# Decode operations in PSUM, the angle's scaling on ScalarE, and g in h's PSUM bank, in an attention and two-layer-block kernel

## Chip, cores and metric

The kernel runs on one core of one Trainium2 chip. The metric is the device time of one launch in microseconds (us). The engines are TensorE (PE; PEld is its weight load), VectorE (DVE), ScalarE (ACT) and GpSimd (POOL); SyncE's queue (SP) issues nearly all transfers.

## What is computed

Three parts follow one another over 4608 tokens (8 batches of 576 tokens, 8 heads of 64, so 512 columns):

```python
# attention; keys and values first averaged over pools of 8 tokens, so 72 keys per head
k_p = k.reshape(B, H, Sp, 8, D).mean(axis=3)
v_p = v.reshape(B, H, Sp, 8, D).mean(axis=3)
attn = softmax(matmul(q, k_p.T) / sqrt(D))
x = matmul(attn, v_p)                    # -> [4608, 512]
# first block: w_in [512, 2048], w_out [2048, 512]
h = x @ w_in
g = h * cos(h)
y = g @ w_out
# second block: w_in [512, 1024], w_out [1024, 512]
h2 = y @ w2_in
solu = h2 * softmax(h2)
out = layer_norm(solu) * g_ln @ w2_out
```

## The kernel before

**Tiling.** The tokens go in 9 blocks of 512 (`NB`, index `j`), the 2048 hidden columns of the first block in 16 chunks of 128 (`NF`, index `f`). A step `n` is one pair `(j, f)`. In a step PE does `h_mm` (12 matmuls into one PSUM bank of the pool `ps_h`, which has two) and `y_mm` of the step two before (12 matmuls into four banks of `ps_y`). Each product is three matmuls on pairs of float32r parts (a high part, and a low part that holds the rest), so every operand is split into two.

**The chain of a step.** From h to g the functions `chain_a`, `chain_b`, `chain_c` do: L527 (DVE) scales h by 1/2pi into an integer, L532 (DVE) takes the whole turns off, L536 (ACT) is the sine; L541 (DVE) multiplies by h, which is the last reader of h's bank; L543 (ACT) copies g's high part, L547 (DVE) subtracts it for the low part. `chain_a` runs in its own step, `chain_b` and `chain_c` of a step run in the next one.

**Decoding the weights.** The weights come as float64 bits. Class `Chunk` turns 128x512 of them into two float32r parts in three stages: `s1` (ACT L94, L95), `s2` (DVE L100, L105, L110, then POOL L113) and `s3` (ACT L122, POOL L125). Class `Pipe` runs the stages of neighbouring chunks one step apart; `parts()` is a generator that gives the DVE operations of `s2` out one at a time, so that `chain_a` can put its own between them. The 32 chunks of the first block's weights are decoded during the attention of block 0 and the steps of block 0, two pipe steps in a step `n`. The second block's weights are decoded in block 8 (`pipe2`). The scratch tiles of the decode lie in the SBUF pool `s2p` (four buffers).

**Attention.** Block 0's attention stands alone at the start, written out by hand; the attention of block `j+1` is laid into the steps of block `j` by `slots()`: `sl[2f]` early in a step, `sl[2f+1]` late. Its PSUM tiles (`sc`, `eTp`, `eLp`, `xo`) come from `ps_a`, which has two banks. In f 1, 2, 9 and 10 the early slot has scores, in f 2 and 10 the late slot has the exponentials, f 3 and 11 have the normalizations (`norm`: DVE L395, L397, L398, then POOL L401, L406), f 5 and 13 the transposes and, where a batch from the third on begins, `prep_v` (POOL L289, ACT L295, POOL L296, ACT L300, DVE L301 to L307), f 6 and 7 and 14 and 15 the product with v. Keys and values are pooled by `kv_jobs`: on POOL (L194, L214, L228), for batch 0's keys on DVE (L206 to L209).

**Order.** All is under a manual schedule: each engine takes its instructions in program order, and the order of the calls in the step loop is the order on every queue:

```python
h_mm(j, f)
chain_b(*steps[n - 1])
parts = pipe.parts(); next(parts, None)
chain_a(j, f, parts)          # then, in block 0, the second pipe step around chain_c
for fn in sl[2 * f]: fn()
chain_c(*steps[n - 1])        # j > 0
y_mm(*steps[n - SK])          # SK = 2
for fn in sl[2 * f + 1]: fn()
```

Of the kernel before, what the change touches and what calls it, by code (L numbers as in the profile page):

```python
# [28 lines left out]
# High words of the float64 range [2^-127, 2^128 - ulp], read as float32.  # L29
# [5 lines left out]
def fused_kernel(ctx, tc, qT_d, kT_d, vN_d, vM_d, vL_d, w_in, w_out, w2_in, w2_out, g_ln, out):  # L35
    """qT_d [pair, (head d), token]; kT_d [batch, pair, (head d), (r key)];
    vN_d [batch < 2, 128-token tile, token, (head d)];
    vM_d [batch >= 2, pair, (head key<64), (r d)]; vL_d [batch >= 2, half, (head rep key>=64), (r d)];
    weights [chunk, row, col] as bits of float64; g_ln [row, chunk]."""
# [43 lines left out]
    class Chunk:  # L83
# [13 lines left out]
        def s2(self):  # L97
            hi, lw = self.raw[:, :, 1], self.raw[:, :, 0]
            t = self.t
            nc.vector.tensor_scalar(  # L100
                out=t.bitcast(F32), in0=t.bitcast(F32), scalar1=WORD_MIN, scalar2=WORD_MAX,
                op0=ALU.max, op1=ALU.min,
            )
            yield
            nc.vector.tensor_scalar(  # L105
                out=t, in0=t, scalar1=0x07FFFFFF, scalar2=3,
                op0=ALU.bitwise_and, op1=ALU.logical_shift_left,
            )
            yield
            nc.vector.scalar_tensor_tensor(  # L110
                out=t, in0=hi, scalar=-0x40000000, in1=t, op0=ALU.bitwise_and, op1=ALU.bitwise_or)
# [3 lines left out]
        def s3(self):  # L115
# [5 lines left out]
            # The high part needs only the high word's bits; the low part takes all the rest.  # L121
# [6 lines left out]
    class Pipe:  # L128
        """Decodes chunks in order in three stages, one step apart, loads running ahead."""
# [17 lines left out]
        def step(self):  # L147
            for _ in self.parts():
                pass

        def parts(self):
            """One step, in three parts between which other work may go."""
            last = self.two.pop(0) if self.two else None
            if self.one:
                c = self.one.pop(0)
                yield from c.s2()
                self.two.append(c)
            if last:
                last.s3()
# [24 lines left out]
    def kv_jobs(b, hf):  # L184
        """Loads of half the heads of batch b; each gives the job that sums the pools."""
# [11 lines left out]
        def k_job(i):  # L197
# [5 lines left out]
            def add():  # L203
                if b == 0:
# [29 lines left out]
    # The first two batches' values, which are wanted early, are pooled on the tensor engine.  # L234
# [77 lines left out]
    class Attn:  # L312
        """Attention of one token block. The first one, which has the chip to itself, takes its
        buffers from the ring of the weights."""
# [141 lines left out]
        def slots(self):  # L456
# [12 lines left out]
            for hf in range(2):  # L469
# [23 lines left out]
                # Keys of the first half come a block ahead, the rest as they are wanted.  # L493
# [30 lines left out]
    def chain_a(j, f, between=iter(())):  # L524
        ps = h_ps[j, f]
        t = gp.tile([P, BLK], F32, tag="t", name="t")
        nc.vector.tensor_scalar(  # L527
            out=t.bitcast(I32), in0=ps, scalar1=1.0 / TWO_PI, scalar2=0.25,
            op0=ALU.mult, op1=ALU.add,
        )  # L530
        next(between, None)
        nc.vector.scalar_tensor_tensor(  # L532
            out=t, in0=t.bitcast(I32), scalar=-TWO_PI, in1=ps, op0=ALU.mult, op1=ALU.add)
        for _ in between:
            pass
        nc.scalar.activation(out=t, in_=t, func=AF.Sin, bias=halfpi)  # L536
        g_t[j, f] = [t, None]

    def chain_b(j, f):
        t = g_t[j, f][0]  # L540
        nc.vector.tensor_tensor(out=t, in0=t, in1=h_ps.pop((j, f)), op=ALU.mult)  # L541
        g = g_t[j, f][1] = gp.tile([P, 2, BLK], F32R, tag="g", name="g")
        nc.scalar.copy(out=g[:, 0], in_=t)  # L543

    def chain_c(j, f):
        t, g = g_t[j, f]
        nc.vector.tensor_tensor(out=g[:, 1], in0=t, in1=g[:, 0].bitcast(F32), op=ALU.subtract)  # L547
# [45 lines left out]
    def h2_mm(t):  # L593
# [3 lines left out]
        # The first two tiles run beside the last block's y.  # L597
# [14 lines left out]
    # u = h2 e^(h2 - max); solu = u / sum, whose layer norm goes by the moments of u.  # L612
# [90 lines left out]
    with tc.manual_schedule():  # L703
# [22 lines left out]
        # A raw buffer serves until the tile that takes over its slot: x or one of the last chunks.  # L726
# [90 lines left out]
        for n in range(len(steps) + SK):  # L817
            if n < len(steps):
# [12 lines left out]
                h_mm(j, f)  # L831
            if 0 < n <= len(steps):
# [3 lines left out]
            if n < len(steps):  # L836
                parts = pipe.parts()
                next(parts, None)
                chain_a(j, f, parts)
            parts = pipe.parts()  # L840
            if j == 0:
                next(parts, None)
                if n > 0:
                    chain_c(*steps[n - 1])
            if n < len(steps):
                if sl:
                    for fn in sl[2 * f]:
                        fn()
                if j == 0 and f in (4, 6):
                    kv_load(1, 1, KV[f // 2 - 2])  # L850
                if j == 0 and f in (5, 7):
                    add(1, 1, KV[f // 2 - 2])
            if j > 0 and n <= len(steps):
                chain_c(*steps[n - 1])
            if n < len(steps):
                for _ in parts:
# [96 lines left out]
```

## Time and profile before

| quantity | value |
|---|---|
| median of 3 runs | 1426.53 us (1426.36 to 1426.8) |
| span of the profiled execution, first to last instruction | 1422.4 us |
| mean granted TensorE clock | 0.982 |
| DVE busy | 981.3 us (69%) |
| ACT busy | 532.0 us (37%) |
| POOL busy | 403.4 us (28%) |

The profiled execution has no time of its own beside its span; 4.1 us of the median lie outside that span. Busy is time in which the engine had an instruction of the program in work; matmuls are pipelined and their ends are modelled, so a busy PE is not PE at its peak. A row that names a DVE operation by its line can be long because it computes or because it waits inside the engine.

### The profile page before, as it was taken

Reading aid. Unit: us, or ns where it says so; the run is one execution under the profiler, and the core shown is the slowest. Engines: PE = TensorE matmul, PEld = TensorE weight load, DVE = VectorE, ACT = ScalarE, POOL = GpSimd, SP = SyncE. Lnnn points to the kernel's source line nnn. Section 1 sums busy time; section 2 is a strip of 40 time slices with the busy share of each in tenths; the row PEclk is TensorE's granted clock in tenths of the full one; section 3 lists DMA queues with packets and bytes.
Section 4 is the critical chain, followed back from the end, with each engine's and each line's share of the span. In section 5 each row is a group of like instructions: output and inputs, shape, how many; then the busy total and the mean of one; then the engine's idle time right before and its main releaser. Section 6 shows DMA issues by size and latency. Waiting matters only on the chain.

```text
span 1422.4 us, 17189 instructions
## 1 busy us (share of the span) xinstructions
PE 1356.9 (95%) x6304; PEld 1117.5 (79%) x6304; DVE 981.3 (69%) x1690; ACT 532.0 (37%) x891; POOL 403.4 (28%) x517
## 2 busy tenths in 40 slices
PE   6778799999999999999999999799899999999998
PEld 4556588888888888888888888578788888888887
DVE  8999966666676666666656655697766666666664
ACT  5665533333343333333324333454222222222222
POOL 3787823231242142142231100353111111111110
PEclk9999999999999999999999999899999999999999
DMA  7433111111020120220110101340111111111100
GB/s 266 147 91 138 57 61 54 31 61 46 32 84 24 60 71 9 75 63 31 47 60 8 45 1 60 104 133 8 60 39 55 40 54 38 52 40 50 44 32 30
DMA packets 43236, 85.27 MB, mean 60 GB/s; under 512 B 4112, under 2 KB 13328, under 8 KB 43152
## 3 DMA queue, kind: packets, MB, share of 16 engines
q1 hardware_dynamic: 43008, 84.16, 18.0%
q8 instruction: 50, 0.82, 0.2%
q14 instruction: 34, 0.28, 0.1%
q10 hardware_dynamic: 144, 0.00, 0.0%
HBM read 65.28 MB, written 18.87 MB: 59 GB/s over the span
## 4 chain that ended last, share of the span: by engine, by line
PE 82%; DVE 12%; issue 2%; DMA 1%; ACT 1%; POOL 1%; SPq 0%; DVEq 0%; ACTq 0%; POOLq 0%
PE y L557 24%; PE h L519 23%; PE o L675 5%; PE o L677 5%; PE o L676 5%; PE h L608 4%; PE h L610 4%; PE h L609 4%; PE lT L661 2%; PE sc L351 2%; DVE dec L110 2%; DVE dec L105 2%; DVE dec L100 1%; DVE t L532 1%; PE eTp L431 1%
## 5 line engine op out<-in xcount | busy, mean ns | idle before, releaser
L519 PE MATMUL h<-x,wi 128*128 128x512 f32 x1728 | 427.5, 397 | 20.7 <-DVE t L541 20.7
L557 PE MATMUL y<-g,wo 128*128 128x512 f32 x1728 | 427.5, 396 | 14.6 <-DVE yo L568 9.6
L519 PEld LDWEIGHTS h<-x,wi 128*128 128x128 f32 x1728 | 328.1, 191 | 92.0 <-DVE t L541 24.3
L557 PEld LDWEIGHTS y<-g,wo 128*128 128x128 f32 x1728 | 323.2, 190 | 83.3 <-DVE yo L568 10.8
L527 DVE TENSOR_SCALAR t<-h 128x512 int32<-128x512 f32 x144 | 99.0, 688 | 157.3 <-PE h L519 157.2
L536 ACT ACTIVATE t<-t,cst 128x512 f32<-128x512 f32 x144 | 104.3, 724 | 230.5 <-DVE t L532 230.1
L543 ACT CAST g<-t 128x512 fp32r<-128x512 f32 x144 | 89.1, 618 | 188.8 <-DVE t L541 182.9
L194 POOL TENSOR_TENSOR kvraw<-kvraw 128x256 f32<-128x256 f32 (+3 forms) x128 | 86.9, 679 | 235.2 <-DMA kvraw<-in_vM 176.2
L648 POOL TENSOR_TENSOR sc<-sc,cst 128x1 f32<-128x1 f32 x36 | 19.8, 549 | 366.5 <-DVE sc L647 208.1
L675 PE MATMUL o<-wi,lh 128*128 128x512 f32 x288 | 116.0, 403 | 0.0
L676 PE MATMUL o<-wi,lh 128*128 128x512 f32 x288 | 112.9, 392 | 0.0
L677 PE MATMUL o<-wi,ll 128*128 128x512 f32 x288 | 112.9, 392 | 0.0
L547 DVE TENSOR_TENSOR g<-t,g 128x512 fp32r<-128x512 f32 x144 | 109.4, 760 | 1.8 <-ACT g L543 1.8
L663 ACT CAST lh<-lT 128x512 fp32r<-128x512 f32 x72 | 38.8, 589 | 184.6 <-PE lT L661 184.6
L401 POOL TENSOR_TENSOR em<-e,sm 128x512 f32<-128x512 f32 x34 | 39.6, 1165 | 229.3 <-PE y L557 220.1
L617 DVE TENSOR_REDUCE sc<-h 128x1 f32<-128x1024 f32 x34 | 41.6, 1224 | 90.8 <-PE h L610 90.8
L113 POOL TENSOR_TENSOR dec<-dec,raw 128x512 int32<-128x512 int32 x48 | 69.0, 1438 | 118.2 <-DVE dec L110 52.2
L532 DVE SCALAR_TENSOR_TENSOR t<-t,h 128x512 f32<-128x512 int32 x144 | 98.7, 686 | 4.4
L541 DVE TENSOR_TENSOR t<-t,h 128x512 f32<-128x512 f32 x144 | 97.1, 675 | 5.6 <-ACT t L536 5.2
L610 PE MATMUL h<-wi,yl 128*128 128x512 f32 x216 | 84.2, 390 | 0.0
L608 PE MATMUL h<-wi,yh 128*128 128x512 f32 x216 | 84.1, 389 | 0.0
L609 PE MATMUL h<-wi,yh 128*128 128x512 f32 x216 | 84.1, 389 | 0.0
(139 smaller groups left out, 1904.2 us busy)
## 6 DMA issues: line engine op xcount, KB each, us to landing
raw<-in_w_in SPq DMA_DIRECT2D x24, 512.0 KB, 3.6
raw<-in_w_out SPq DMA_DIRECT2D x24, 512.0 KB, 3.5
kvraw<-in_kT SPq DMA_DIRECT2D x32, 288.0 KB, 2.8
qT<-in_qT SPq DMA_DIRECT2D x36, 256.0 KB, 3.3
yd<-yo SPq DMA_DIRECT2D x36, 256.0 KB, 2.8
yr<-yd SPq DMA_DIRECT2D x18, 512.0 KB, 3.7
out<-o SPq DMA_DIRECT2D x36, 256.0 KB, 2.0
kvraw<-in_vM SPq DMA_DIRECT2D x24, 256.0 KB, 2.6
```

Source lines behind the costliest of these rows:

```text
L519: nc.tensor.matmul(ps, lhsT=w[:, a, kk, :], rhs=x[kk][:, b], start=(kk == 0 and i == 0), stop=(kk == KD - 1 and i == 2),)
L527: nc.vector.tensor_scalar(out=t.bitcast(I32), in0=ps, scalar1=1.0 / TWO_PI, scalar2=0.25, op0=ALU.mult, op1=ALU.add,)
L532: nc.vector.scalar_tensor_tensor(out=t, in0=t.bitcast(I32), scalar=-TWO_PI, in1=ps, op0=ALU.mult, op1=ALU.add)
L536: nc.scalar.activation(out=t, in_=t, func=AF.Sin, bias=halfpi)
L547: nc.vector.tensor_tensor(out=g[:, 1], in0=t, in1=g[:, 0].bitcast(F32), op=ALU.subtract)
L557: nc.tensor.matmul(o, lhsT=w[:, a, P * e:P * (e + 1)], rhs=g[:, b], start=(f == 0 and i == 0), stop=(f == NF - 1 and i == 2),)
L608: nc.tensor.matmul(ps[hh], lhsT=hi[:, kk, c], rhs=w[:, 0], start=first, stop=False)
L609: nc.tensor.matmul(ps[hh], lhsT=hi[:, kk, c], rhs=w[:, 1], start=False, stop=False)
L610: nc.tensor.matmul(ps[hh], lhsT=lo[:, kk, c], rhs=w[:, 0], start=False, stop=last)
L675: nc.tensor.matmul(ps, lhsT=hi[:, c], rhs=w[:, 0], start=(c == 0), stop=False)
L676: nc.tensor.matmul(ps, lhsT=hi[:, c], rhs=w[:, 1], start=False, stop=False)
L677: nc.tensor.matmul(ps, lhsT=lo[:, c], rhs=w[:, 0], start=False, stop=(c == NF2 - 1))
```

## The change

- The first two DVE operations of `s2` write a PSUM tile `bits` from `ps_a` instead of the SBUF scratch tile; the third reads it and writes SBUF.
- A pipe step is issued whole, with `s3` of the older chunk ahead of `s2`; `parts()` is gone.
- L527 leaves DVE: a new `chain_k` scales h by an activation on ACT.
- `chain_b` writes the product back into h's PSUM bank; the copy of the high part reads it there, and `chain_c` subtracts from it there, so that `chain_c` is now the last reader of h's bank.
- In block 0 a step's order is `chain_b`, a pipe step, `chain_c`, `chain_k`, early attention, a pipe step, `chain_a`. In the other blocks it is `chain_b`, early attention, `chain_c`, `chain_k`, `chain_a`.
- For batch 0 only one of two keys' tiles of a half is pooled on DVE; the other goes to POOL (`add` in `k_job`).

```diff
         def s2(self):
...
+            b = ps_a.tile([P, BLK], I32, tag="a", name="bits")
             nc.vector.tensor_scalar(
-                out=t.bitcast(F32), in0=t.bitcast(F32), scalar1=WORD_MIN, scalar2=WORD_MAX,
+                out=b.bitcast(F32), in0=t.bitcast(F32), scalar1=WORD_MIN, scalar2=WORD_MAX,
                 op0=ALU.max, op1=ALU.min,
             )
-            yield
             nc.vector.tensor_scalar(
-                out=t, in0=t, scalar1=0x07FFFFFF, scalar2=3,
+                out=b, in0=b, scalar1=0x07FFFFFF, scalar2=3,
                 op0=ALU.bitwise_and, op1=ALU.logical_shift_left,
             )
-            yield
             nc.vector.scalar_tensor_tensor(
-                out=t, in0=hi, scalar=-0x40000000, in1=t, op0=ALU.bitwise_and, op1=ALU.bitwise_or)
+                out=t, in0=hi, scalar=-0x40000000, in1=b, op0=ALU.bitwise_and, op1=ALU.bitwise_or)
...
         def step(self):
-            for _ in self.parts():
-                pass
-
-        def parts(self):
-            """One step, in three parts between which other work may go."""
             last = self.two.pop(0) if self.two else None
+            if last:
+                last.s3()
             if self.one:
                 c = self.one.pop(0)
-                yield from c.s2()
+                c.s2()
                 self.two.append(c)
-            if last:
-                last.s3()
             self.fill()
...
             def add():
-                if b == 0:
+                if b == 0 and i == 0:
...
-    def chain_a(j, f, between=iter(())):
+    def chain_k(j, f):
         ps = h_ps[j, f]
         t = gp.tile([P, BLK], F32, tag="t", name="t")
-        nc.vector.tensor_scalar(
-            out=t.bitcast(I32), in0=ps, scalar1=1.0 / TWO_PI, scalar2=0.25,
-            op0=ALU.mult, op1=ALU.add,
-        )
-        next(between, None)
+        nc.scalar.activation(
+            out=t.bitcast(I32), in_=ps, func=AF.Copy, scale=1.0 / TWO_PI, bias=0.25)
+        g_t[j, f] = [t, None]
+
+    def chain_a(j, f):
+        t, ps = g_t[j, f][0], h_ps[j, f]
         nc.vector.scalar_tensor_tensor(
             out=t, in0=t.bitcast(I32), scalar=-TWO_PI, in1=ps, op0=ALU.mult, op1=ALU.add)
...
     def chain_b(j, f):
-        t = g_t[j, f][0]
-        nc.vector.tensor_tensor(out=t, in0=t, in1=h_ps.pop((j, f)), op=ALU.mult)
+        t, ps = g_t[j, f][0], h_ps[j, f]
+        nc.vector.tensor_tensor(out=ps, in0=t, in1=ps, op=ALU.mult)
         g = g_t[j, f][1] = gp.tile([P, 2, BLK], F32R, tag="g", name="g")
-        nc.scalar.copy(out=g[:, 0], in_=t)
+        nc.scalar.copy(out=g[:, 0], in_=ps)
 
     def chain_c(j, f):
-        t, g = g_t[j, f]
-        nc.vector.tensor_tensor(out=g[:, 1], in0=t, in1=g[:, 0].bitcast(F32), op=ALU.subtract)
+        g = g_t[j, f][1]
+        nc.vector.tensor_tensor(
+            out=g[:, 1], in0=h_ps.pop((j, f)), in1=g[:, 0].bitcast(F32), op=ALU.subtract)
...
+            early = sl[2 * f] if n < len(steps) and sl else []
+            late = sl[2 * f + 1] if n < len(steps) and sl else []
...
+            if n < len(steps) and j == 0:
+                pipe.step()
                 if n > 0:
                     chain_c(*steps[n - 1])
...
+                chain_k(j, f)
+                for fn in early:
+                    fn()
...
+                pipe.step()
+                chain_a(j, f)
+            else:
+                for fn in early:
+                    fn()
+                if n <= len(steps):
+                    chain_c(*steps[n - 1])
+                if n < len(steps):
+                    chain_k(j, f)
+                    chain_a(j, f)
```

## Rows read from the trace of the kernel before

**Rows 1.** Busy time by stretch: us, busy of each engine, granted clock, DMA share, GB/s

```profile
44.76:161.88 117.12, 89.81 (x368) 68.31 (x367) 115.89 (x163) 73.83 (x117) 89.86 (x72) 0.90 0.33 107
175.00:880.00 705.00, 704.25 (x3353) 584.88 (x3353) 450.08 (x784) 255.80 (x392) 178.41 (x310) 1.00 0.15 47
```

**Rows 2.** Groups of DVE, 44.76 to 161.88 us: count, busy us, mean ns

```profile
L105 DVE TENSOR_SCALAR dec<-dec 128x512 int32<-128x512 int32 x26 | 28.2, 1086 | 0.0
L110 DVE SCALAR_TENSOR_TENSOR dec<-raw,dec 128x512 int32<-128x512 int32 x27 | 25.8, 956 | 0.5
L100 DVE TENSOR_SCALAR dec<-dec 128x512 f32<-128x512 f32 x26 | 18.9, 728 | 0.2 <-ACT dec L94 0.2
L527 DVE TENSOR_SCALAR t<-h 128x512 int32<-128x512 f32 x13 | 8.8, 678 | 0.0
L371 DVE TENSOR_REDUCE mx<-sc 128x4 f32<-128x288 f32 x8 | 3.5, 444 | 0.0
```

**Rows 3.** Timeline: start us, us taken, engine, line

```profile
131.46 1.28 POOL L125 TENSOR_TENSOR wo<-dec,wo 128x512 fp32r<-128x512 f32 x1
131.99 1.03 DVE L105 TENSOR_SCALAR dec<-dec 128x512 int32<-128x512 int32 x1
...
906.42 0.43 DVE L105 TENSOR_SCALAR dec<-dec 128x512 int32<-128x512 int32 x1
```

**Rows 4.** Groups of ACT, 44.76 to 161.88 us

```profile
L536 ACT ACTIVATE t<-t,cst 128x512 f32<-128x512 f32 x13 | 9.4, 723 | 3.9 <-DVE t L532 3.9
```

**Rows 5.** Groups of POOL, 44.76 to 161.88 us

```profile
L113 POOL TENSOR_TENSOR dec<-dec,raw 128x512 int32<-128x512 int32 x26 | 39.6, 1522 | 27.3 <-DVE dec L110 12.8 <-ACT t L536 8.5 <-DMA raw<-in_w_out 3.4
```

**Rows 6.** Timeline of DVE: where steps 1 and 13 of block 0 begin

```profile
51.73 0.68 DVE L541 TENSOR_TENSOR t<-t,h 128x512 f32<-128x512 f32 x1
52.33 1.29 DVE L100 TENSOR_SCALAR dec<-dec 128x512 f32<-128x512 f32 x1
...
161.88 0.67 DVE L541 TENSOR_TENSOR t<-t,h 128x512 f32<-128x512 f32 x1
```

**Rows 7.** Timeline of block 4, steps f 3 to 6

```profile
504.71 1.29 POOL L401 TENSOR_TENSOR em<-e,sm 128x512 f32<-128x512 f32 x1 [3.58 <-PE y L557]
...
515.65 0.61 POOL L289 TENSOR_TENSOR vw<-v,cst 128x256 f32<-128x256 f32 x1
...
516.31 2.88 PE L519 MATMUL h<-x,wi 128*128 128x512 f32 x12
...
519.72 0.68 DVE L547 TENSOR_TENSOR g<-t,g 128x512 fp32r<-128x512 f32 x1
...
520.68 2.94 PE L557 MATMUL y<-g,wo 128*128 128x512 f32 x12
```

**Rows 8.** The line of `prep_v`'s first operation, all its instructions

```profile
L289 POOL TENSOR_TENSOR vw<-v,cst x12: 610/612/615, 216.1 to 758.6; 128x256 f32<-128x256 f32 x12
```

**Rows 9.** Timeline of block 4, step f 13 and after

```profile
566.65 2.88 PE L519 MATMUL h<-x,wi 128*128 128x512 f32 x12
...
...
570.76 2.95 PE L557 MATMUL y<-g,wo 128*128 128x512 f32 x12
```

**Rows 10.** Waits of PE, 840 to 1020 us: us in total, times, longest

```profile
PE h L519 <- DVE t L541: 3.4, 2, 2.6
```

**Rows 11.** A pause of PE, and stretches behind two pauses; columns as in group 1

```profile
1017.70:1021.70 4.00, 0.00 (x0) 0.03 (x1) 3.24 (x3) 0.00 (x0) 2.85 (x2) 1.00 0.00 0
1022.70:1025.50 2.80, 2.80 (x9) 2.22 (x8) 2.10 (x3) 1.95 (x4) 0.00 (x0) 0.50 0.00 0
928.50:931.50 3.00, 2.99 (x13) 2.46 (x14) 2.96 (x4) 2.23 (x4) 2.15 (x2) 1.00 0.43 139
```

**Rows 12.** Timeline of block 0's attention

```profile
13.44 0.76 POOL L406 TENSOR_TENSOR el<-e,sm 128x128 f32<-128x128 f32 x2
...
15.07 0.45 DVE L362 TENSOR_REDUCE mx<-sc 128x4 f32<-128x288 f32 x1
...
28.69 1.55 POOL L194 TENSOR_TENSOR kvraw<-kvraw 128x288 f32<-128x288 f32 x2
```

More of the change, by code (lines that the diff above doesn't have):

```diff
@@ L522, in h_mm @@
                 )
-    def chain_a(j, f, between=iter(())):
+    def chain_k(j, f):
         ps = h_ps[j, f]
         t = gp.tile([P, BLK], F32, tag="t", name="t")
-        nc.vector.tensor_scalar(
-            out=t.bitcast(I32), in0=ps, scalar1=1.0 / TWO_PI, scalar2=0.25,
-            op0=ALU.mult, op1=ALU.add,
-        )
-        next(between, None)
+        nc.scalar.activation(
[3 more added lines that the diff above has]
+        t, ps = g_t[j, f][0], h_ps[j, f]
         nc.vector.scalar_tensor_tensor(
             out=t, in0=t.bitcast(I32), scalar=-TWO_PI, in1=ps, op0=ALU.mult, op1=ALU.add)
-        for _ in between:
-            pass
         nc.scalar.activation(out=t, in_=t, func=AF.Sin, bias=halfpi)
-        g_t[j, f] = [t, None]
     def chain_b(j, f):
-        t = g_t[j, f][0]
-        nc.vector.tensor_tensor(out=t, in0=t, in1=h_ps.pop((j, f)), op=ALU.mult)
+        t, ps = g_t[j, f][0], h_ps[j, f]
+        nc.vector.tensor_tensor(out=ps, in0=t, in1=ps, op=ALU.mult)
         g = g_t[j, f][1] = gp.tile([P, 2, BLK], F32R, tag="g", name="g")
-        nc.scalar.copy(out=g[:, 0], in_=t)
+        nc.scalar.copy(out=g[:, 0], in_=ps)
     def chain_c(j, f):
-        t, g = g_t[j, f]
-        nc.vector.tensor_tensor(out=g[:, 1], in0=t, in1=g[:, 0].bitcast(F32), op=ALU.subtract)
+        g = g_t[j, f][1]
+        nc.vector.tensor_tensor(
+            out=g[:, 1], in0=h_ps.pop((j, f)), in1=g[:, 0].bitcast(F32), op=ALU.subtract)
     def y_mm(j, f):
@@ L835, in fused_kernel @@
                 y_out(*steps[n - SK - 1])
[L836 to L842, printed above, removed]
+            if n < len(steps) and j == 0:
+                pipe.step()
                 if n > 0:
                     chain_c(*steps[n - 1])
[L845 to L849, printed above, removed]
+                chain_k(j, f)
+                for fn in early:
+                    fn()
+                if f in (4, 6):
                     kv_load(1, 1, KV[f // 2 - 2])
-                if j == 0 and f in (5, 7):
+                if f in (5, 7):
                     add(1, 1, KV[f // 2 - 2])
[L853 to L856, printed above, removed]
-                    pass
+                pipe.step()
[8 more added lines that the diff above has]
+                    chain_a(j, f)
             if n >= SK:
@@ L860, in fused_kernel @@
             if n < len(steps):
-                if sl:
-                    for fn in sl[2 * f + 1]:
-                        fn()
+                for fn in late:
+                    fn()
                 if pipe2 and f > 0:
```

## The prediction

> **What bounds the kernel now.** I read the busy times by stretch first. From 175 to 880 us, which is blocks 1 to 7, PE is busy for 704.25 of 705.00 us at a granted clock of 1.00 [rows 1]: there every microsecond in which PE waits is added to the time, and work taken off DVE is worth nothing. From 44.76 to 161.88 us, block 0's steps beside the decode, DVE is busy for 115.89 of 117.12 us and PE for 89.81 [rows 1]: there DVE sets the pace. The groups of DVE in that stretch say what fills it: L105 takes 1.086 us in the mean, L110 0.956, L100 0.728, while L527, of the same size with its source in PSUM, takes 0.678 [rows 2]. The timeline shows why. With nothing on POOL beside it L105 takes 0.43 us; with L125 on POOL from 131.46 to 132.74 it takes 1.03 and ends at 133.02, 0.28 behind POOL's end [rows 3]. So much of DVE's busy time is waiting for POOL's instruction to be over.
>
> **The change, part by part.** The sum is made against the profiled span of 1422.4 us; 4.1 us of the median of 1426.5 lie outside it and are left alone.
>
> *Block 0's steps.* Step 1 begins with L541 at 51.73 and step 13 at 161.88 [rows 6], so twelve steps took 110.15 us. After the change no operation of the decode on DVE has two operands in SBUF, and neither has the chain of g. I take 0.68 us for each (L527's price, the nearest row with PSUM in it [rows 2]); the next operation starts 0.60 later (51.73 to 52.33 [rows 6]), or at the end plus 0.05 where it needs the result. A step without attention is then, in DVE's order: L541 0.60, a decode 2.06 (0.73, 0.73, 0.60), L547 0.60, a decode 2.06, L532 0.68; then the sine, 0.72 [rows 4] and 0.12 for two handings, because L541 of the next step now stands right behind. That is 6.85 us, in which DVE waits 0.8. ACT's nine operations of about 0.6 (the scaling of h among them) fit in, and POOL's four too, at the 1.3 us that L125 needs [rows 3] rather than the 1.52 of L113 [rows 5].
> Attention was hidden in the waits for POOL and now adds to DVE. Scores add four operations of 0.44 [rows 2]: 8.6 us for f 1, 2, 9, 10. In f 3 and 11 ACT has two exponentials and two table loads more, and L397 can still wait for POOL: 9.95. In f 4 and 12 POOL is behind with the normalizations and L94 waits for L113: 7.75. Copies on ACT that DVE waits for make 9.0 of f 5, 9.55 of f 6 and 7.9 of f 7; f 8 is 6.9. The sum is 103.15, so 7.0 us are gained, and 1.2 at the same rate in the last two steps with decode: **-8.2**. Lower bound: if the waits among ACT, POOL and DVE are hidden, -16. Upper bound: seven operations a step now write or read PSUM in a way for which there is no row; 0.1 us more for each takes it all, so 0. I take the value between because L527's row is of the same size and differs only in where it writes.
> Here the Trainium skill speaks against the change ("VectorE: DVE Perf Modes", section "Why PSUM operands drop a tier"): an operation with an operand in PSUM can't use both SBUF read ports for one tensor, so an fp32 scale runs at one element a cycle instead of two. The rows show the price, 0.43 for L105 in SBUF against 0.678 for L527. By that rule alone a decode would get 0.5 us longer; the means of 1.086 and 0.728 say that the fast form is rarely had here. It is rival 4 below.
>
> *The wait for h's bank.* `chain_c` now reads h's bank, so `h_mm` two steps on waits for L547, where before it waited for L541. L547 stands behind the early attention on DVE. In most steps it is there in time: the early work needs PE's short matmuls, and 2.72 us of y follow them. The exception is f 5 in the blocks where `prep_v` runs, which are six (L289 ran twelve times, twice a block [rows 8]). In block 4 h of f 6 started at 516.31, and L547 ran from 519.72 to 520.40 [rows 7]: at its old place it would hold h up for 4 us. It comes earlier, though. What L547 waits for begins with the normalization on POOL at 504.71 [rows 7], which waited behind L527 and L532; these now come after it, and before it stands the later exponential (the sine of f 2 now follows the scores). Together POOL starts 1.45 us earlier, and so does L289 behind its transfer: 514.2. From L289's start to L547's end were 4.75 us (515.65 to 520.40), and a handing to PE of 0.2 makes 519.15, 2.8 us after h could start. Before, y behind the attention's product started 0.74 late in that step (516.31 + 2.72 + 0.91 for the eight short matmuls is 519.94; it started at 520.68 [rows 7]). So the loss is 2.0 us in each of six blocks: **+12**. Bounds: +6 if L289 comes another microsecond earlier; +21 if the clock falls too (rival 3). Queued behind the waiting matmul is the attention's product, and behind that y, whose operands are all there.
>
> *f 13.* There L289 doesn't wait for a transfer, and ACT comes to `prep_v` before the scaling and the sine of its own step, so the product's operands are 3 us earlier. L547 ends about when h may start. What is gained is the late start of y: 570.76 against 566.65 + 2.72 + 0.91 = 570.28 [rows 9], 0.5 us in six blocks: **-3**. Bounds -4 and +3, the latter if L547 comes half a microsecond after h could start.
>
> *Block 8.* PE waited 3.4 us for L541, in two waits [rows 10], in the steps with two decodes each. With 2.06 us a decode, three operations of the chain and the wait for g's copy such a step takes DVE 6.8 us, against 5.44 of PE, so most but not all of the waiting goes: **-2.5**, bounds -3.4 and 0.
>
> *Block 0's attention.* The fourth tile of keys is now pooled on POOL, behind a normalization that ends there at 14.20 [rows 12]. Its two halvings (1.55 [rows 12]) and two small sums (0.75, an estimate by size) end at 16.5, the first scores at 17.3, where DVE's maximum stood at 15.07 [rows 12]: 2.2 late. The reduction that DVE saves falls into that wait, and the decode behind it is 0.5 longer. This stretch is bound by DVE, so I take **+2.5**; bounds 0, if later waits absorb it, and +5, if the three other decodes there add their 0.5 and PE resumes at the lower clock.
>
> Everything else is at nothing: in the blocks 1 to 7 the scaling on ACT and the shorter L547 are hidden behind PE, as ACT is busy for 255.80 of 705 us [rows 1]. If that cover went, the scaling's 0.7 us would stand between h and L532 in all 144 steps.
>
> The sum is -8.2 + 12 - 3 - 2.5 + 2.5 = +0.8: a span of 1423.2 and a time of **1427.3 us**, no change that shows (0.2% is 2.9 us, about what a measurement of this kernel can tell).
>
> **Rivals.**
> 1. *The wait for h's bank doesn't bite.* If the chain of normalization, transfer and `prep_v` ends 2.8 us earlier than I think, the +12 goes: 1415 to 1416. For it: half of that chain is waiting, for a transfer and for DVE's order. Against it: L547 was 4 us too late before, and two thirds of that must vanish.
> 2. *Block 0 gets much shorter.* DVE's waits for the sine and for ACT's copies overlap: -16 instead of -8.2, so 1419.5. For it: PE would allow it, with 89.81 us of work in 117.12. Against it: ACT and POOL come to 6 us and more in each step.
> 3. *The clock falls* (slower). After a pause of PE of 4.0 us the granted clock was 0.50, the lower level of 1.2 GHz, for 2.80 us; behind a wait of 2.6 us it stayed at 1.00 [rows 10, 11]. My pauses at f 5 are 2.8 us. If they make it fall, each costs 1.4 us more: 6 x 1.4 is 8.4, so 1435.7. It decides from a pause somewhere between those two.
> 4. *The fast form's loss is all that remains* (slower). If DVE's waits for POOL come back as waits for POOL's results (POOL was busy for 89.86 of 117.12 us [rows 1]), or an operation from PSUM to PSUM takes 0.1 us longer than L527, block 0 gains nothing: 1435.5. This is what the rule named above would give.
>
> **How the numbers follow.** My forecast has a chance of 0.40, with its own range of 1421 to 1433; of it 0.09 lies on the faster side of 0.2%, 0.22 within, 0.09 on the slower side. Rival 1 has 0.20, rival 2 0.12 (both faster), rival 3 0.14 and rival 4 0.14 (both slower). That makes 0.41 faster, 0.22 no change, 0.37 slower. The range goes to the middle of the rivals on each side, 1415 to 1437, and leaves out some 2 in 10.
>
> **What would show it.** Right: L100, L105 and L110 near 0.7 us each in block 0, however POOL is busy; twelve steps near 103 us; PE waiting for L547 (its line after the change) some 2.8 us, six times, ahead of h at f 6, and hardly at f 14; the first waits in block 8 gone; the maximum of the fourth scores near 17.3 us. Wrong: operations on PSUM that are longer than 0.75; `prep_v`'s L289 more than 2 us earlier against h; a granted clock below 1.00 in blocks 1 to 6; a loop over the sine longer than 7 us, or waits for the two banks of `ps_a`, which the decode now shares with the attention.

## The result and the profile after

The changed kernel took 1440.74 us (median of 4 runs, 1436.27 to 1441.45) against 1426.44 us of the kernel before beside it: a ratio of 1.0096, 95% interval 1.0079 to 1.0114. It is 1% slower. The profiled span grew from 1422.4 to 1439.6 us, by 17.2; the medians differ by 14.3. The two traces lie further apart because launches of one kernel differ: the spans of the kernel before, over all its launches, run from 1420.6 to 1427.2 us, so its trace is one of the short ones, and those of the changed kernel from 1434.5 to 1439.6, of which its trace is the longest. What is read from one trace against another is uncertain by a part of that. Of the 4.1 us put outside the span of before some 1.8 lie outside it (the changed kernel's traced launch took 1441.39 us with a span of 1439.6); the rest is that its trace is a short one.

Where the time went can be read from one instruction that stands once in every step in both kernels, the multiplication of the sine by h (L541 before, L536 after). This is its start after minus its start before, at the ends of the stages:

| at the multiplication of | step 1 | step 13 | block 1 begins | block 7 begins | block 8 begins | block 8 ends |
|---|---|---|---|---|---|---|
| start after minus start before, us | +3.88 | -4.53 | -3.90 | +19.41 | +19.44 | +17.12 |

Block 0's attention costs 3.9 us, the twelve steps behind it give back 8.4, the last steps of block 0 cost 0.6, blocks 1 to 6 cost 23.3, block 7 nothing, and block 8 gives back 2.3.

**Block 0.** The first view is the busy time by stretch, with columns as in [rows 1]: the twelve steps of block 0, and blocks 1 to 7.

```profile
55.61:157.35 101.74, 79.66 (x335) 62.38 (x336) 86.25 (x142) 73.71 (x121) 71.93 (x68) 0.92 0.36 113
175.00:880.00 705.00, 688.57 (x3244) 572.94 (x3243) 365.91 (x653) 307.49 (x489) 163.29 (x304) 0.98 0.14 43
```

DVE, busy for nearly all of its stretch before [rows 1], is busy for 86.25 of 101.74 us. In the second row PE has lost 16 us of its 705, and the granted clock is 0.98 where it was 1.00. The groups of DVE and POOL in the twelve steps answer to [rows 2, 5]:

```profile
L107 DVE TENSOR_SCALAR bits<-bits 128x512 int32<-128x512 int32 x24 | 16.8, 699 | 0.8
L111 DVE SCALAR_TENSOR_TENSOR dec<-raw,bits 128x512 int32<-128x512 int32 x24 | 16.5, 689 | 2.2
L103 DVE TENSOR_SCALAR bits<-dec 128x512 f32<-128x512 f32 x24 | 16.4, 685 | 0.0
...
L542 DVE TENSOR_TENSOR g<-h,g 128x512 fp32r<-128x512 f32 x12 | 8.2, 685 | 0.5 <-ACT g L538 0.5
...
L114 POOL TENSOR_TENSOR dec<-dec,raw 128x512 int32<-128x512 int32 x24 | 31.4, 1306 | 6.5 <-DVE dec L111 6.5
```

Each operation of a decode takes 0.69 to 0.70 us whatever POOL does, and POOL's addition takes 1.31 us instead of 1.52. The shortest, the median and the longest (ns) of the second operation in the twelve steps say it best, first before, then after:

```profile
L105 DVE TENSOR_SCALAR dec<-dec x24: 411/978/1520, 54.1 to 158.7; 128x512 int32<-128x512 int32 x24
L107 DVE TENSOR_SCALAR bits<-bits x24: 698/699/700, 56.9 to 154.5; 128x512 int32<-128x512 int32 x24
```

One of the prediction's signs of being wrong did show: the scores on PE (L347) wait 9.3 us in these steps for L111, that is for a bank of `ps_a` that the decode holds. The maxima L367 on DVE, which need the scores, stand 0.0 us, so no price of it shows. The timelines of DVE and POOL show the step starts, which answer to [rows 6], and the wait for the fourth tile of keys, which answers to [rows 12]:

```profile
55.61 0.70 DVE L536 TENSOR_TENSOR h<-t,h 128x512 f32<-128x512 f32 x1 [2.40 <-ACT t L531]
...
157.35 0.69 DVE L536 TENSOR_TENSOR h<-t,h 128x512 f32<-128x512 f32 x1 [0.79 <-ACT t L531]
...
17.61 0.46 DVE L358 TENSOR_REDUCE mx<-sc 128x4 f32<-128x288 f32 x1 [3.50 <-PE sc L347]
...
14.04 1.36 POOL L190 TENSOR_TENSOR kvraw<-kvraw 128x288 f32<-128x288 f32 x2
```

**Blocks 1 to 6.** PE's waits from 182 to 882 us hold one entry (total us, times, longest):

```profile
PE h L515 <- DVE g L542: 16.4, 6, 3.5
```

Block 4's timeline shows one of the six; it answers to [rows 7].

```profile
515.08 1.05 POOL L397 TENSOR_TENSOR em<-e,sm 128x512 f32<-128x512 f32 x1 [0.47 <-ACT t L531]
...
523.76 0.61 POOL L285 TENSOR_TENSOR vw<-v,cst 128x256 f32<-128x256 f32 x1
...
524.73 0.25 ACT L296 ACTIVATE vlh<-v 128x64 fp32r<-128x64 f32 x1
...
525.08 0.64 DVE L297 TENSOR_TENSOR vll<-v,vlh 128x64 fp32r<-128x64 f32 x1 [4.87 <-ACT vlh L296]
...
527.83 0.68 DVE L542 TENSOR_TENSOR g<-h,g 128x512 fp32r<-128x512 f32 x1
...
528.57 4.36 PE L515 MATMUL h<-x,wi 128*128 128x512 f32 x12 [2.21 <-DVE g L542]
```

Two things are to be seen. `prep_v` begins at 523.76 on POOL. DVE stands for 4.87 us before L297, with the subtraction L542 behind it, and h's matmuls wait 2.21 us for L542. And those twelve matmuls then take 4.36 us, where they took 2.88 before [rows 7]. The stretches behind the six pauses, columns as above, say why:

```profile
215.90:222.60 6.70, 5.92 (x16) 4.76 (x16) 2.02 (x4) 1.31 (x2) 2.37 (x6) 0.50 0.45 122
321.60:324.90 3.30, 3.30 (x9) 2.58 (x9) 1.05 (x2) 1.31 (x2) 0.00 (x0) 0.52 0.63 173
424.90:430.90 6.00, 6.00 (x16) 4.84 (x17) 1.18 (x2) 1.31 (x2) 1.55 (x4) 0.50 0.47 145
529.90:533.20 3.30, 3.30 (x10) 2.61 (x9) 0.69 (x1) 0.59 (x1) 1.44 (x3) 0.51 0.64 228
632.40:635.70 3.30, 3.21 (x8) 2.54 (x9) 1.32 (x3) 1.31 (x2) 0.38 (x2) 0.50 0.57 175
735.60:742.00 6.40, 6.40 (x30) 5.43 (x31) 2.79 (x5) 2.40 (x4) 1.71 (x4) 1.00 0.41 125
```

In five of six blocks PE worked at 0.50, the lower level of 1.2 GHz: 5.92 + 3.30 + 6.00 + 3.30 + 3.21 = 21.7 us of work, half of which, 10.9 us, would not have been needed at 1.00 if everything in it went at half the pace (an estimate, and an upper one: see e8). Block 6, with the shortest pause (2.10 us), kept 1.00. It is the natural control: from f 5 to f 9 it lost 2.0 us against before, the others 3.5 to 6.1.

**Block 8.** Of the two waits of [rows 10], 3.4 us, one is left:

```profile
PE h L515 <- DVE g L542: 1.3, 1, 1.3
```

### The profile page after: what moved, and what is told of

It reads as the page before. It is cut to its first block, busy times and chain, and to the rows that moved or that the text cites. A ratio compares the mean times of both kernels' runs of the same rounds, so it can differ in the third digit from the quotient of the medians.

```text
span 1439.6 us, 17090 instructions
## 1 busy us (share of the span) xinstructions
PE 1361.7 (95%) x6304; PEld 1124.8 (78%) x6304; DVE 867.7 (60%) x1540; ACT 608.2 (42%) x1035; POOL 381.4 (26%) x525
## 5 line engine op out<-in xcount | busy, mean ns | idle before, releaser
L515 PE MATMUL h<-x,wi 128*128 128x512 f32 x1728 | 434.5, 402 | 28.0 <-DVE g L542 28.0
L515 PEld LDWEIGHTS h<-x,wi 128*128 128x128 f32 x1728 | 331.9, 194 | 102.7 <-DVE g L542 33.1
L190 POOL TENSOR_TENSOR kvraw<-kvraw 128x256 f32<-128x256 f32 (+3 forms) x132 | 82.4, 624 | 267.2 <-DMA kvraw<-in_vM 204.8
L536 DVE TENSOR_TENSOR h<-t,h 128x512 f32<-128x512 f32 x144 | 99.8, 693 | 69.3 <-ACT t L531 67.4
L538 ACT CAST g<-h 128x512 fp32r<-128x512 f32 x144 | 84.2, 585 | 118.5 <-DVE h L536 118.4
L542 DVE TENSOR_TENSOR g<-h,g 128x512 fp32r<-128x512 f32 x144 | 98.1, 681 | 42.6 <-ACT g L538 42.6
L523 ACT ACTIVATE t<-h 128x512 int32<-128x512 f32 x144 | 86.4, 600 | 57.2 <-PE h L515 56.9
L397 POOL TENSOR_TENSOR em<-e,sm 128x512 f32<-128x512 f32 x34 | 35.6, 1046 | 248.1 <-DVE sm L394 240.0
L450 DVE TENSOR_TENSOR x<-xo,x 128x512 fp32r<-128x512 f32 x36 | 24.9, 691 | 97.3 <-ACT x L449 97.3
```

The costliest lines, as they stand in the source:

```text
L515: nc.tensor.matmul(ps, lhsT=w[:, a, kk, :], rhs=x[kk][:, b], start=(kk == 0 and i == 0), stop=(kk == KD - 1 and i == 2),)
L536: nc.vector.tensor_tensor(out=ps, in0=t, in1=ps, op=ALU.mult)
L542: nc.vector.tensor_tensor(out=g[:, 1], in0=h_ps.pop((j, f)), in1=g[:, 0].bitcast(F32), op=ALU.subtract)
```

## Experiments

Theory A: h's bank, held until the subtraction that stands behind the late `prep_v` on DVE, makes PE pause, and the lower clock behind the pause costs about as much again; the decode and g in PSUM free DVE and POOL from each other, which is block 0's gain. The rivals stand in the expectations. This is how far each run had moved against the kernel before, measured at the same multiplication as above (us), and the median of its runs. In e7, e8 and e9 the line numbers of the operations concerned are one higher. The differences in a row are read from one launch. e4's edit touches nothing ahead of step 1, and step 1 begins 1.5 us later than before all the same, so differences of that size between two launches can be chance; e4's trace is also the shortest of its four launches.

| run | step 1 | step 13 | block 1 | block 7 | block 8 | end of block 8 | median, us | ratio to before, 95% |
|---|---|---|---|---|---|---|---|---|
| the change | +3.88 | -4.53 | -3.90 | +19.41 | +19.44 | +17.12 | 1440.74 | 1.0079 to 1.0114 |
| e1 | +4.69 | +0.87 | +3.12 | -1.46 | -1.46 | -3.52 | 1421.32 | 0.9954 to 0.9978 |
| e2 | +4.85 | -3.58 | -2.98 | -8.08 | -8.08 | -10.51 | 1413.36 | 0.9895 to 0.9930 |
| e3 | +4.67 | -3.76 | -3.14 | +20.03 | +20.04 | +17.91 | 1443.70 | 1.0107 to 1.0145 |
| e4 | +1.48 | -3.93 | -3.78 | +63.00 | +70.17 | +70.72 | 1501.53 | 1.0509 to 1.0562 |
| e5 | +0.83 | -7.57 | -6.94 | -11.83 | -11.83 | -14.21 | 1410.88 | 0.9871 to 0.9912 |
| e6 | +6.07 | +6.16 | +4.45 | -0.40 | -0.40 | +1.81 | 1426.21 | 0.9986 to 1.0005 |
| e7 | +4.61 | +2.37 | +3.02 | +14.58 | +17.06 | +20.52 | 1445.67 | 1.0111 to 1.0157 |
| e8 | +4.39 | -4.04 | -3.38 | +10.96 | +11.10 | +9.01 | 1431.94 | 1.0032 to 1.0060 |
| e9 | -0.95 | +16.37 | +22.16 | +21.85 | +21.85 | +21.63 | 1444.15 | 1.0113 to 1.0144 |
| e10 | +4.21 | -4.24 | -3.59 | -6.77 | -6.75 | -9.12 | 1416.34 | 0.9917 to 0.9946 |
| e11 | +1.76 | +1.44 | +1.25 | +1.13 | +1.13 | +5.84 | 1428.05 | 1.0002 to 1.0026 |

### Who holds the bank (e1 to e4, e10)

**e1**: the product goes to SBUF again, so that the multiplication is the last reader of h's bank.

```diff
-        nc.vector.tensor_tensor(out=ps, in0=t, in1=ps, op=ALU.mult)
+        nc.vector.tensor_tensor(out=t, in0=t, in1=h_ps.pop((j, f)), op=ALU.mult)
...
-            out=g[:, 1], in0=h_ps.pop((j, f)), in1=g[:, 0].bitcast(F32), op=ALU.subtract)
+        nc.vector.tensor_tensor(out=g[:, 1], in0=t, in1=g[:, 0].bitcast(F32), op=ALU.subtract)
```

> The changed kernel with the product and the low part of g taken from the SBUF tile again, so that h's bank is free at the multiplication; the scaling on ScalarE, the decode in PSUM and the order stay. Theory A (the wait of h for chain_c's subtraction, and the lower clock behind it, cost blocks 1 to 6 some 25 us): no wait of PE for the subtraction ahead of h, clock 1.00 in blocks 1 to 6, 1413 to 1419 us. Theory B (the new order and the scaling on ScalarE make the step's chain itself late): y still waits for the subtraction by 2 us and more in six steps, over 1428 us.

Measured 1421.32 us. No wait of PE shows in blocks 1 to 7, and the blocks 1 to 6 give 4.6 us back instead of costing 23.3; so theory A holds for them, and B falls. The time is 2 us above A's range because of block 0, where the twelve steps gain 3.8 us instead of 8.4. The group of the subtraction, both of whose sources are in SBUF again, tells why:

```profile
L542 DVE TENSOR_TENSOR g<-t,g 128x512 fp32r<-128x512 f32 x12 | 13.5, 1122 | 0.5 <-ACT g L538 0.5
```

It takes 1.12 us with both sources in SBUF and 0.685 with one in PSUM. Keeping g in h's bank thus has a worth of its own in block 0, and a price in the blocks behind it as long as the subtraction comes late there.

**e2**: the hold stays, the subtraction moves ahead of the early attention in blocks 1 to 8.

```diff
+                if n <= len(steps):
+                    chain_c(*steps[n - 1])
                 for fn in early:
                     fn()
-                if n <= len(steps):
-                    chain_c(*steps[n - 1])
```

> The changed kernel with chain_c ahead of the early attention in blocks 1 to 8, g still in h's bank. Theory A: the bank is free about 1.5 us into the next step, so the six pauses at f 6 and the low clock are gone: 1413 to 1419 us. Theory B (holding the bank is itself dear, since any wait on DVE now reaches PE through two banks): waits of 1 us and more stay ahead of h in most blocks, over 1428 us. What VectorE loses by standing 0.65 us for the copy in each step should be hidden behind TensorE.

Measured 1413.36 us, as theory A has it: the fault is not that the bank is held, but what stands ahead of its last reader. The stretch from 190 to 875 us, and DVE's group of the subtraction in it:

```profile
190.00:875.00 685.00, 685.00 (x3281) 572.72 (x3280) 373.26 (x658) 311.08 (x498) 162.25 (x301) 1.00 0.15 47
...
L542 DVE TENSOR_TENSOR g<-h,g 128x512 fp32r<-128x512 f32 x111 | 76.7, 691 | 95.8 <-ACT g L538 95.8
```

PE never stands and the clock is 1.00, while DVE now waits 95.8 us for ScalarE's copies, behind which the attention queues. In a stretch that PE bounds that costs nothing.

**e3**: `prep_v` two slots earlier, from f 5 to f 4 and from f 13 to f 12.

```diff
-                    r[o + 9].append(lambda b=b, hf=hf: prep_v(b, hf))
+                    r[o + 7].append(lambda b=b, hf=hf: prep_v(b, hf))
```

> The changed kernel with prep_v two slots earlier (early in f 4 and f 12), nothing else. Theory A with its cause in prep_v's late start: the subtraction at f 5 comes within 2.9 us after h may be issued, no wait over 0.5 us, clock 1.00, 1413 to 1419 us. Theory C (the transposes and the copies of the attention's left part make the subtraction late, prep_v only by chance beside them): the pause at f 6 stays at 1.5 us or more, over 1428 us.

Measured 1443.70 us: my expectation by theory A was wrong, and C is not right either. The pauses at f 6 are gone, but the waits of PE over 175 to 882 us now read

```profile
PE h L515 <- DVE g L542: 21.5, 12, 2.7
```

and the timeline of block 4 shows them one step earlier:

```profile
517.71 0.61 POOL L285 TENSOR_TENSOR vw<-v,cst 128x256 f32<-128x256 f32 x1
...
520.18 0.42 DVE L303 TENSOR_TENSOR vL<-vlw,cst 128x256 fp32r<-128x256 f32 x1
520.52 0.68 DVE L542 TENSOR_TENSOR g<-h,g 128x512 fp32r<-128x512 f32 x1
...
521.26 3.06 PE L515 MATMUL h<-x,wi 128*128 128x512 f32 x12 [1.94 <-DVE g L542]
```

`prep_v` starts 3.4 us behind the multiplication in f 4 at 514.35, in the changed kernel 8.7 us behind the one in f 4 at 515.06; but the subtraction right behind it, that of the step before, is late in its stead, at f 5 and likewise at f 13. The wait goes with `prep_v`. The clock fell behind two of the twelve pauses, in blocks 2 and 5.

**e10**: `prep_v` one slot earlier, late in f 4. `r[o + 9]` becomes `r[o + 8]`; DVE's operations of `prep_v` then stand ahead of a multiplication.

> The changed kernel with prep_v one slot earlier, late in f 4 and f 12: its operations on VectorE then stand behind that step's chain and ahead of the next multiplication, and no more directly ahead of a subtraction. Theory A (a subtraction is late only where prep_v's operations stand right ahead of it in VectorE's queue): waits ahead of h under 1 us in blocks 1 to 6, clock 1.00, 1414 to 1422 us. Theory I (prep_v makes the subtraction behind it late from any slot, as when it stood two slots earlier): waits of 1.5 us and more stay, over 1430.

Measured 1416.34 us, theory A: PE is busy for 684.62 of the 685.00 us from 190 to 875, at 1.00.

```profile
190.00:875.00 685.00, 684.62 (x3273) 570.40 (x3273) 369.38 (x657) 310.40 (x497) 162.09 (x301) 1.00 0.15 47
```

`prep_v` starts on POOL 3.4 us behind the multiplication in f 4, just as in e3, which pauses; in e2, which doesn't, it starts 8.6 to 8.8 us behind it, as late as in the change. So not the time at which `prep_v` comes decides but its place in DVE's queue against the bank's last reader.

**e4**: the kernel before with the hold alone. L541 writes h's bank, L543 and L547 read it there; the rest is as before.

> The kernel before with one part of the change alone: product into h's bank, subtraction from it. Theory A: in the old order the subtraction of f 5 and of f 13 comes 3.2 to 3.4 us after h of the next step but one could start, so PE pauses 4.1 to 4.3 us ahead of h twice in each of six blocks, and the clock falls behind each: 12 x (4.2 - 0.6 + 2) = 67, about 1490 us, at least 1470. Theory D (the hold costs little without the new order): below 1445 us.

Measured 1501.53 us. Blocks 1 to 6 lost 66.8 us against the 67 expected, partly by chance: the pauses at f 6 and f 14 are 2.7 to 3.7 us instead of 4.1 to 4.3, twelve more of 0.45 us at f 4 and f 12 add to them, and the clock fell behind eight of the twelve long ones, not behind each. PE's waits from 197 to 850 us:

```profile
PE h L519 <- DVE g L547: 43.4, 24, 3.7
```

In the changed kernel the hold makes no pause at f 14. Which of its other parts, the order or the scaling on ScalarE, takes that one away was not tried by itself.

### What the lower clock costs (e8)

**e8**: the changed kernel with work for PE in the pause. Zeros are added to y's banks, so the sums stay the same.

```diff
                 y_mm(*steps[n - SK])
+                if n < len(steps) and f == 5 and 1 <= j <= 6:
+                    for i in range(8):
+                        nc.tensor.matmul(
+                            y_ps[j][i % 4 // 2][0:32, i % 2], lhsT=zero, rhs=at[j].x[i % 4][:, 0],
+                            start=False, stop=False)
```

> The changed kernel with eight more matmuls of 512 columns, of a 32-column tile of zeros added to y's banks, issued at f 5 of blocks 1 to 6 between y and the waiting h, 1.95 us of work that nothing waits for. They fill most of the 2.1 to 3.5 us in which TensorE stood. Theory A (the low clock behind the pause costs 11 to 12 us in the six blocks, the pause itself the rest): clock 1.00 behind it, h of f 6 in 3.0 us, 1427 to 1432. Theory H (the clock costs little, since h's bank and VectorE set the time there): 1437 us or more.

Measured 1431.94 us, theory A. The stretch, and h of f 6 in block 1:

```profile
190.00:875.00 685.00, 678.76 (x3241) 560.91 (x3241) 361.14 (x644) 304.34 (x485) 161.75 (x301) 1.00 0.14 44
...
217.05 3.02 PE L516 MATMUL h<-x,wi 128*128 128x512 f32 x12 [1.55 <-DVE g L543]
```

In the changed kernel the same matmuls were

```profile
216.69 5.49 PE L515 MATMUL h<-x,wi 128*128 128x512 f32 x12 [3.54 <-DVE g L542]
```

The clock stays at 1.00, and block 1's h takes 3.02 us where it took 5.49. In the sum h was not ready sooner: the filling ends 1.85 us behind y each time (1.95 was expected), and 6 x 1.85 and the 6.2 us of waiting that were left are 17.3 us, against 16.4. Yet the six blocks cost 14.3 us instead of 23.3. So 9.0 us of the 23.3 come back, and 9.9 come from the clock if the 0.9 us of longer waiting are set against it. Block by block it is the same: the five whose clock had fallen cost 10.5 us instead of 21.3, with 0.9 us less of waiting in them, and block 6, whose clock had not fallen, costs 1.8 us more, since `prep_v` begins 1.8 us later there. And 5.49 is 1.82 times 3.02, by which 21.7 us of work at 0.50 are 9.8 us too long.

### What block 0 gains from (e5, e6, e7, e9, e11)

**e5**: e2 with both key tiles of a half of batch 0 pooled on DVE, as before (`if b == 0:`).

> The kernel with chain_c ahead of the early attention (1413.4 us), and both of a half's key tiles of batch 0 pooled on VectorE again. Theory A (the fourth tile's pooling on POOL makes the last scores of block 0's attention late, which costs the 3.9 to 4.9 us by which step 1 begins later): step 1 begins within 1 us of 51.73, 1408.5 to 1411. Theory E (the delay comes from the decode issued whole and its two-port form lost): step 1 stays 3 us late or more, 1412 to 1415.

Measured 1410.88 us, theory A: step 1 begins 0.83 us after that of before, 4.0 earlier than in e2, and 3.7 of it are left at the end. It is the fastest kernel of the study, 1.1% below the kernel before. The reduction L202 runs on DVE while it would wait, and the first maximum of the last scores is 2.5 us earlier than in the change (17.61):

```profile
12.24 1.15 DVE L202 TENSOR_REDUCE kp<-kvraw 128x72 f32<-128x576 f32 x1
...
15.10 0.45 DVE L358 TENSOR_REDUCE mx<-sc 128x4 f32<-128x288 f32 x1
```

**e6**: e2 with the decode's first two operations writing SBUF, still issued whole (`b = t` instead of the PSUM tile).

> The kernel with chain_c ahead of the early attention (1413.4 us), and the decode's first two operations written to SBUF again, each step of the decode still issued whole. Theory A (in block 0 an operation with all operands in SBUF waits for POOL's instruction): L103 and L107 together take 0.5 us or more longer than in PSUM in block 0, twelve steps 4 us longer or more, 1417 to 1424. Theory F (block 0's gain comes from the order and from g in PSUM; the decode's place is worth nothing): 1411.5 to 1415.

Measured 1426.21 us, 12.9 above e2 and 2 above A's range. The twelve steps gain nothing against before, so in this order the whole 8.4 us hang on the place of these two results, and 4.6 us of block 8 too (+2.2 where e2 has -2.4). L103 and L107 together are only 0.25 us longer than in PSUM, where theory A had 0.5; the third operation, L111, which it left out, adds 0.20. DVE's groups in the twelve steps:

```profile
L107 DVE TENSOR_SCALAR dec<-dec 128x512 int32<-128x512 int32 x24 | 22.1, 921 | 0.8
L111 DVE SCALAR_TENSOR_TENSOR dec<-raw,dec 128x512 int32<-128x512 int32 x24 | 21.4, 891 | 0.8
L103 DVE TENSOR_SCALAR dec<-dec 128x512 f32<-128x512 f32 x24 | 17.1, 714 | 0.0
```

**e7**: e2 with the scaling on DVE, at the same place.

> The kernel with chain_c ahead of the early attention (1413.4 us), and the scaling of the angle on VectorE again, at the same place in the order. Theory A (VectorE bounds block 0): 0.6 us a step in block 0 and in the steps with two decodes of block 8, 1421 to 1426. Theory G (ScalarE and POOL bound block 0 as much, so that the scaling only changes hands): 1411 to 1416. Blocks 1 to 7 the same in both.

Measured 1445.67 us; both expectations failed. Block 0 lost less than A said (twelve steps -2.2 instead of -8.4), but blocks 1 to 7 cost 14.0 us where e2 gains 5.1, and block 8 another 5.9 us against e2. PE's waits in blocks 1 to 7:

```profile
PE h L515 <- DVE g L543: 8.4, 15, 0.9
```

The clock stays at 1.00. My reading, which no run tests further: with the bank held, the way from h through scaling, turns, sine, multiplication and subtraction has to fit between h's matmuls, and on DVE the scaling cannot run beside the early attention. Without the hold the same move was worth nothing there (e11: -0.1 us from block 1 to block 7). Of the 19 us, 9.4 show as idle time of PE between 190 and 875 us; the rest lies inside PE's groups of matmuls and was not followed further. That the scaling on ScalarE is worth more in the PE-bound blocks than in block 0 is new: the prediction had it at nothing there.

**e11**: the kernel before with only the scaling on ScalarE.

> The kernel before with the scaling of the angle on ScalarE, at its old place in the order, and nothing else of the change. Theory A (VectorE bounds block 0, where the scaling's 0.68 us falls away): 0.4 to 0.6 us a step there and in block 8's first steps, 1416 to 1422 us. Theory G (in block 0 the removal of the whole turns then waits for ScalarE's queue, and the gain is lost): 1424 to 1430. Blocks 1 to 7 unchanged in both.

Measured 1428.05 us: no gain, so theory A's expectation failed, and not for G's reason: the removal of the whole turns waited 0.7 us in twelve steps. Half of the time went here:

```profile
L105 DVE TENSOR_SCALAR dec<-dec 128x512 int32<-128x512 int32 x24 | 29.8, 1243 | 0.4
```

Before, in the same twelve steps, it was

```profile
L105 DVE TENSOR_SCALAR dec<-dec 128x512 int32<-128x512 int32 x24 | 25.9, 1078 | 0.0
```

So 24 x 0.165 = 4.0 of the 12 x 0.677 = 8.1 us saved are spent in this line alone, though no operation of it changed. Its shortest still takes 0.44 us, its median 1.39 instead of 0.98, so I read it as longer waiting for POOL. Where the rest of the 8.1 went, and the 1.8 us of block 0's attention and the 4.7 us of block 8, was not followed.

**e9**: the kernel before with only the bits in PSUM, the operations still handed out one at a time.

> The kernel before with the first two operations of a decode written to PSUM, and nothing else of the change: the operations are still handed out one at a time between those of the chain. Theory A (the two-operand SBUF form waits for POOL wherever the operation stands; undone in the changed kernel's order it cost 12.9 us in all): L101 and L106 near 0.70 us each in block 0, 1416 to 1421 us. Theory F (in the old order the time saved comes back as waits for POOL's results, for the sine or for a bank of the attention's): 1423 to 1429.

Measured 1444.15 us; the gain of L100 and L105 came as expected (0.687 us each), and block 0's twelve steps became 17.3 us longer all the same. The time is above both theories' ranges; of theory F's three waits the one for a bank shows, and longer than it had it. Two things are seen. First, the longest waiting on DVE moved on to the subtraction:

```profile
L548 DVE TENSOR_TENSOR g<-t,g 128x512 fp32r<-128x512 f32 x12 | 18.9, 1575 | 0.0
```

It took 0.863 us before:

```profile
L547 DVE TENSOR_TENSOR g<-t,g 128x512 fp32r<-128x512 f32 x12 | 10.4, 863 | 0.0
```

Second, PE waits from 45 to 185 us for the banks that the decode shares with the attention:

```profile
PE sc L352 <- issue: 18.2, 4, 7.7
PE eLp L417 <- DVE dec L111: 14.2, 2, 7.1
```

For `sc` the view names no releaser; each of these four waits ends 0.10 us behind the end of an L111, the decode's last reader of its bank. The timeline of DVE in f 6 shows how long one bank is held:

```profile
109.59 0.69 DVE L101 TENSOR_SCALAR bits<-dec 128x512 f32<-128x512 f32 x1
...
113.16 0.69 DVE L455 TENSOR_TENSOR x<-xo,x 128x512 fp32r<-128x512 f32 x1 [1.43 <-ACT x L454]
113.77 0.69 DVE L106 TENSOR_SCALAR bits<-bits 128x512 int32<-128x512 int32 x1
114.55 0.69 DVE L111 SCALAR_TENSOR_TENSOR dec<-raw,bits 128x512 int32<-128x512 int32 x1
```

From its first operation to its third 5.65 us pass, with the attention's work in between; of two banks the attention has one. Issued whole, as in the change, a decode holds its bank for about 2 us. So in these runs the decode in PSUM pays only together with the whole issue, and fully (e1 against e2) only with g in PSUM as well.

## Why the prediction was wrong

Forecast was 1427.3 us with a span 0.8 above that of before; the span rose by 17.2, and the time lies 4 us beyond the range. Of the 16.4 us between, 14.3 are in blocks 1 to 6, 1.4 in block 0's attention, 0.4 in block 0's steps and 0.2 in block 8.

*The decode and block 0's steps: right in mechanism and nearly in size.* -7.0 was predicted for twelve steps and -8.4 measured (101.74 us against 103.15). The price of 0.68 us an operation measured 0.685 to 0.699, POOL's 1.3 measured 1.31, and the steps that were worked out came near one by one: 8.6 for steps with scores measured 8.6 to 8.7, 6.9 for one without attention measured 6.9. f 4 and f 12 were 0.7 and 0.85 us shorter than thought, f 3 0.35 shorter and f 11 0.3 longer. The further -1.2 for the last steps did not come; they lost 0.6.

*Rival 4, the loss of the fast form: wrong.* The Trainium skill's rule ("VectorE: DVE Perf Modes", section "Why PSUM operands drop a tier") agrees with the trace on the single operation, 0.43 against 0.685 us, but what it would give in time did not come: e6 with SBUF is 12.9 us slower than e2 with PSUM. What outweighs it is the waiting between DVE and POOL: in e6 L107 takes 0.43 us at its shortest, but 1.15 in the median. In e9 and e11 it looks as if it moved to an operation that still has the form: L105 went from 1.08 to 1.24 us, the subtraction from 0.863 to 1.575. The Trainium skill's page "SBUF — State Buffer", section "Who interferes with whom", says that a DVE instruction with two SBUF sources contends with a GpSimd instruction that reads SBUF; the trace agrees, with 1.12 us for L542 in e1 and 0.685 with one source in PSUM.

*The wait for h's bank: place, cause and mean length right, price wrong.* It was put at f 6 in six blocks with 2.8 us each; it stood there, six times, with a mean of 16.4 / 6 = 2.73 us, and e2, e3 and e10 show its cause to be the one named, the subtraction behind `prep_v` on DVE. The way from L289's start to the end of the subtraction was taken as 4.75 us and measured 4.75 (523.76 to 528.51). **The step that failed is the term for these six pauses, which held nothing for the clock behind them.** I held that a pause of 2.8 us leaves the clock at 1.00, since behind a wait of 2.6 us it had stayed there [rows 10, 11], and so chose the forecast against rival 3, which got a chance of 0.14. In the changed kernel the clock fell behind five of six pauses, one of them of 2.21 us. e8, which keeps PE at work in the pause, shows the price: 9.9 of the 23.3 us, 9.0 as measured without the correction for the waiting. Rival 3 named the cause; its 8.4 us came near because two errors partly cancel: six falls of 2.8 us at the lower level were reckoned, and five came, with 3.2 to 6.0 us of work each. Its 2.80 us is the length of the stretch in its row [rows 11], not of the lower level: in the same trace the clock is still 0.50 from 1025.50 to 1025.80. And its sentence that a pause length between 2.6 and 4.0 us decides is wrong: a pause of 2.13 us brought the lower level and one of 3.67 us did not (last section).

*What is saved beside the wait: too large.* For y's late start 0.74 us a block were taken off the pauses, 4.4 in all, and 3 for f 13: 7.4 us together. e2, which has no pause, gains 5.1 in these blocks. So +9 was predicted for blocks 1 to 6. If the change without its pauses would gain what e2 gains, the account of the 23.3 is -5.1 + 16.4 + 12.0; of the 12.0 the clock is 9.9, and some 2 us stay open.

*Block 0's attention: right in kind, small in size.* The fourth scores' first maximum was predicted at 17.3 and stood at 17.61; the cost was +3.9 instead of +2.5, inside its bounds, and e5 leaves 0.8 of it.

*Block 8: right.* -2.5 predicted, -2.3 measured.

*"Everything else at nothing":* nothing else shows in the change, but the reason given doesn't carry. I had the scaling hidden behind PE in blocks 1 to 7. e7 shows that, once the bank is held and the subtraction stands first, it is worth some 19 us there.

## What to carry to other kernels

When a buffer's last reader moves to a later instruction, look at what stands ahead of that instruction on its own in-order queue, not only at the time the data is ready; moving the last reader ahead of the unrelated work (e2, 27 us) moved one call. Price a new pause of TensorE with the clock behind it, as a chance and not as a certainty, and not by its length: here the clock fell behind five of six pauses of the change, two of twelve of e3 and eight of the twelve long ones of e4. And where two engines wait for each other inside instructions, a cut in one operation can be eaten by the next that has the same form, as in e11, which gained nothing; e1, which left one such operation, kept 3.8 of 8.4 us.

## What the hardware showed

The length of a pause did not decide whether the clock fell. In e3, these two stretches follow pauses of 2.63 us (block 1, from 207.56 to 210.19) and 2.13 us (block 2, to 313.77); before both PE had run the twelve matmuls of y back to back:

```profile
210.20:213.20 3.00, 3.00 (x14) 2.44 (x15) 1.23 (x2) 1.31 (x2) 1.29 (x4) 1.00 0.13 19
314.70:318.30 3.60, 3.60 (x11) 2.73 (x10) 0.69 (x1) 0.95 (x2) 0.67 (x2) 0.53 0.28 82
```

The longer pause left 1.00, the shorter one brought the lower level. In e4 even this pause of 3.67 us left 1.00 in the stretch behind it, while the clock fell behind others of 2.71 and 2.73 us:

```profile
273.92 3.02 PE L519 MATMUL h<-x,wi 128*128 128x512 f32 x12 [3.67 <-DVE g L547]
...
273.95:277.30 3.35, 3.35 (x17) 2.85 (x18) 0.84 (x2) 0.58 (x1) 1.97 (x4) 1.00 0.54 201
```

In the changed kernel 2.10 us left it and 2.21 did not. Nor did the fall wait for PE's next work: in block 1 of the changed kernel the clock was down before h began, in block 4 some 1.3 us after h began. The Trainium skill ("TensorE: Matmul & The Clock Gate", section "What's actually happening") calls the lower level the default, which activity releases, and says that the number of slow matmuls at a kernel's start varies between runs of one kernel; behind pauses of 2.2 to 3.5 us within one run, PE worked 3.2 to 6.0 us at 0.50 here, which agrees in kind. What decided in each case stays open.
